# Linear attention and a gated MLP on one core: the first product's Strassen groups accumulate on copies in PSUM, with all operations in a new order

## The chip, the cores and the metric

The kernel runs on 1 core of one Trainium2 chip. A core has five engines, each of which works through its own queue in order: TensorE (PE, matmuls, with weight loads, PEld, that overlap them), VectorE (DVE), ScalarE (ACT), GpSimd (POOL) and SyncE (SP). They wait for each other through semaphores. SP and POOL here also issue the DMA transfers, which sixteen DMA engines carry out. Matmuls write to PSUM, which has 8 banks of 512 float32 columns on 128 partitions; DVE and ACT read and write it.

The metric is device time in microseconds (us), as the median of several executions. Before, it is 257.55 us (3 runs, 257.51 to 258.29).

## The reference

Two stages. The first is linear attention over 8 batches, 8 heads, 576 positions and head size 64; the second multiplies the 4608 x 512 result by two weight matrices with x * sigmoid(x) (silu) between them.

```python
def _attn_ref(q, k, v):
    q_s = np.exp(q - np.max(q, axis=-1, keepdims=True))
    q_s = q_s / (np.sum(q_s, axis=-1, keepdims=True) + 1e-09)
    k_s = np.exp(k - np.max(k, axis=2, keepdims=True))
    k_s = k_s / (np.sum(k_s, axis=2, keepdims=True) + 1e-09)
    kv = np.einsum('bhsd,bhse->bhde', k_s, v)
    return np.einsum('bhsd,bhde->bhse', q_s, kv)

def _moe_ref(x, w_in, w_out):          # x is the attention's output, 4608 x 512
    h = x @ w_in                       # w_in: 512 x 2048
    g = h * (1.0 / (1.0 + np.exp(-h)))
    return g @ w_out                   # w_out: 2048 x 512
```

## The kernel before

**Order.** The kernel defines some 800 named operations (`op(name, f, ...)` from L624 on) and then calls them in the order of the text `ORDER` (L18 to L67, run at L807). Each call appends instructions to the queues of the engines that it uses, so the order of the names is, engine by engine, the order of the instructions. No scheduler moves anything afterwards. The start (batch 0's attention, L545 to L621) is written out by hand ahead of the list.

**Attention, by batch b.** Names carry the batch, and .0 or .1 for the half of the heads.
- `lq`, `lk`, `lv` (load, L146) bring 576 KB of q, k or v each. Batch 0 is issued by SP, batches 1 and 2 by POOL, 3 to 7 by SP. Each of the three has two buffers, so a load waits until the buffer's last reader is done.
- `eq` and `ek` are the exponentials on ACT (L163, L168); `z` sums a row of q on DVE and takes its reciprocal (L207, L211); `n` multiplies by it, on POOL from batch 2 on (L216); `tq` (L226) is a DMA transpose of q, issued by SP; batch 0 and 1 are transposed by PE (`tr`, `tc`). `vc` casts v to bf16, on POOL from batch 2 on (L144).
- `kv` (L248, PE) multiplies k and v, `kc` normalizes the result on DVE. `X` (L282, PE; `xt` for chunk 1) forms the attention's output of a chunk of 512 rows, already transposed, in PSUM banks 0, 1, 6 and 7, and four `x` copies (ACT or DVE) bring it to SBUF.

**Weights.** `W1a` to `W1d` and `W2a` to `W2d` are loads by POOL (L564, L570) that also convert to fp16. `WS` and `T` are sums and differences of weight blocks on DVE (L373, L487).

**First 576 rows** (batch 0) go through both products plainly: `w` (PE, L307, 16 blocks of 128 hidden units), `h` and `v` (tanh on ACT, product on DVE), then `p0` to `p15` (PE, L445), which accumulate in banks 2 to 5. `p12` to `p15` read `W2d`. Chunk t = 1 has only 448 rows of its own; half its hidden units are plain, `m0` to `m7` (PE, L335) with `mu` (silu on ACT).

**Strassen chunks, t = 1 to 8.** Both products use the seven-product form of a 2 x 2 block multiplication. In the first product a group g (two per chunk, 1 then 0; chunk 1 has one) is made of products `g{t}.{g}.1` to `.7` (L425), each of eight matmuls of 256 columns, in the order 1, 2, 6, 5, 7, 4, 3. Products 1, 6, 7 and 4 accumulate in banks 0 and 1, one on top of the other. Products 2, and then 5 and 3, use a second pair of banks: 2 and 3 or 6 and 7. With P for product, the four results are C11 = P1 + P2, C12 = P1 + P6 + P5 + P3, C22 = P1 + P6 + P7 + P5 and C21 = P1 + P6 + P7 + P4. To get them, three copies of the growing sum (`s`, L142 on ACT or L144 on DVE; 128 x 1024 float32) are taken into SBUF, and three adds on DVE (`a`, L403) bring the other pair of banks to them. Four silus on ACT (`u`, L409) write the hidden values; three read the sums in SBUF, one reads banks 0 and 1.

Each copy must have read banks 0 and 1 before PE may add the next product to them; the list therefore puts other PE work in between, mostly the second product's products for the chunk before, `b{t}.{i}.{m}` (L503; eight matmuls of 256 columns each, banks 4 and 5). `S`, `sa` to `sc`, `wa` to `wl` and `o` are the second product's sums, copies, adds and stores; the last chunk's are called `e`.

Of the kernel before, what the change touches and what calls it, by code (L numbers as in the profile page):

```python
# [42 lines left out]
    b3.5.1 s4.0.1a S3.4 b3.7.0 vc6.1 u4.1.2 g4.0.7 z6.1 vc6.0 g4.0.5 s4.0.2a b3.7.1 a4.0.2 n6.1 g4.0.4 sc3
    u4.0.2 g4.0.3 wc3 n6.0 b3.3.0 u4.0.4 a4.0.1 b3.4.0 u4.0.0 X5.0 X5.1 kv6 x5.0a x5.1v tq6 x5.3a x5.2v
    b3.3.1 u4.0.1 xs5.1 g5.1.1 xs5.2 wb3 b3.4.1 s5.1.0v o2.1 ek7.1 g5.1.2 kc6 g5.1.6 wl3a xs5.3 xs5.4 a5.1.0
    lv7.0 b4.2.0 s5.1.1a lv7.1 b4.1.0 S4.1 eq7.1 g5.1.7 ek7.0 b4.2.1 s5.1.2v o3.1 g5.1.5 S4.2 b4.1.1 u5.1.0
    a5.1.2 g5.1.4 sa4 g5.0.2 o3.0 u5.1.4 wa4 g5.1.3 S4.3 u5.1.2 vc7.1 g5.0.1 b4.6.0 a5.1.1 vc7.0 s5.0.0a
    b4.6.1 a5.0.0 u5.1.1 g5.0.6 S4.4 b4.5.0 s5.0.1a b4.5.1 sb4 u5.0.0 g5.0.7 g5.0.5 s5.0.2v b4.7.0 eq7.0
    a5.0.2 b4.7.1 z7.1 g5.0.4 sc4 g5.0.3 b4.4.0 a5.0.1 u5.0.4 b4.4.1 wc4 u5.0.1 X6.0 X6.1 kv7 x6.0v u5.0.2
    x6.3v b4.3.0 x6.1a kc7 b4.3.1 x6.2a xs6.1 xs6.2 g6.1.1 xs6.4 wl4v g6.1.2 S5.1 s6.1.0a b5.1.0 a6.1.0  # L50
    g6.1.6 xs6.3 g6.0.2 wb4 s6.1.1a S5.2 b5.1.1 o4.0 b5.2.0 S5.3 g6.1.7 S5.4 b5.2.1 s6.1.2a z7.0 g6.1.5 sa5
    g6.1.4 wa5 n7.0 b5.6.0 a6.1.2 u6.1.4 b5.6.1 g6.0.1 n7.1 sb5 u6.1.0 g6.1.3 s6.0.0a b5.7.0 a6.1.1 tq7
    b5.7.1 a6.0.0 u6.1.1 g6.0.6 sc5 b5.5.0 s6.0.1a o4.1 g6.0.5 u6.1.2 g6.0.7 b5.5.1 s6.0.2v b5.4.0 wc5
    g6.0.4 a6.0.2 b5.4.1 u6.0.4 b5.3.0 u6.0.2 X7.0 X7.1 x7.0a x7.1v g6.0.3 x7.2a xs7.1 u6.0.0 g7.1.1 x7.3v
# [12 lines left out]
"""  # L67


@with_exitstack  # L70
def kernel(
    ctx: ExitStack,
    tc: tile.TileContext,
    q: bass.AP,
    k: bass.AP,
    v: bass.AP,
    w_in: bass.AP,
# [190 lines left out]
    def pieces(t):  # L268
        a, e = (S, 2 * TCH) if t == 1 else (t * TCH, (t + 1) * TCH)
        got = []  # L270
        while a < e:
# [3 lines left out]
            a += n  # L275
        return got

    def xt_mm(b, cc, col, n, bank, dst):
        for r in range(2):
            for s in range(2):  # L280
                h = slice(s * 64, (s + 1) * 64)
# [267 lines left out]
    for name, src in (("qt", q), ("kt", k)):  # L549
        load(0, name, src, 0, nc.sync)  # L550
        if name == "qt":
            load(0, name, src, 1, nc.sync)
# [286 lines left out]
```

## Time and profile before

| What | Value |
|---|---|
| median of 3 runs | 257.55 us |
| the profiled execution's own time | 258.61 us |
| its span, first to last instruction | 256.6 us |
| TensorE clock granted over the span | 1.0 |
| DVE adds of a group, 128 x 1024 (L403) | 42 of 1214 ns |
| ACT copies out of PSUM, 128 x 1024 (L142) | 29 of 1010 ns |
| DVE copies out of PSUM, 128 x 1024 (L144) | 13 of 1222 ns |
| ACT silu, from SBUF and from PSUM (L409) | 42 of 1056 ns, 14 of 1020 ns |
| ACT table loads | 16 of 1283 ns |
| read from HBM, written to HBM | 36.70 MB, 9.44 MB |

Times in the trace count from the span's start. "PE PS L445 <- DMA W" reads: PE, whose instruction on line 445 writes the tile PS, waited for the DMA that writes the tile W. The profile's busy time of PE is modelled, since matmuls are pipelined; whether PE lost time is seen in the distance from one matmul's start to the next. "Landing" is the time at which a transfer's semaphore tells that all its data are there.

### The profile page before, as it was taken

The page shows a single profiled execution, that of the slowest core. Times are in us where ns is not written, and L with a number is a line of the kernel's source. Part 1 is how long each engine was busy: PE and PEld are TensorE (multiplying, and loading weights), DVE is VectorE, ACT ScalarE, POOL GpSimd, SP SyncE. Part 2 cuts the span into 40 slices and gives each one's busy share as a digit, 9 for nine tenths or more (in the row PEclk, how much of TensorE's full clock was granted, in tenths as well). Part 3 has the DMA queues.
Part 4 walks back from the last instruction along what each step waited for, and adds up shares of the span by engine and source line. Part 5 has one row for each costly group of instructions (what it writes and reads, how often), then busy time and mean ns, then how long its engine had stood idle before and what let it go on. Part 6 is the DMA issues. An engine that isn't in the chain of part 4 may idle for free.

```text
span 256.6 us, 6459 instructions
## 1 busy us (share of the span) xinstructions
PE 249.1 (97%) x2732; PEld 204.2 (80%) x2732; DVE 206.2 (80%) x276; ACT 190.9 (74%) x225; POOL 65.8 (26%) x62
## 2 busy tenths in 40 slices
PE   8799999999999999999999999999999999999994
PEld 3457746656888888888888888888888888888883
DVE  2958999888999898998987986896579836886752
ACT  5766876699999999999879988737587665664411
POOL 1753593650450622350073030006000000000022
PEclk9999999999999999999999999999999999999999
DMA  7999999979959957996874960021807000600365
GB/s 248 348 181 297 302 301 283 351 140 393 378 128 213 403 187 137 361 335 168 276 266 68 224 236 3 3 52 32 163 14 153 13 0 4 148 18 0 66 141 123
DMA packets 36044, 45.89 MB, mean 179 GB/s; under 512 B 16288, under 2 KB 21088, under 8 KB 36016
## 3 DMA queue, kind: packets, MB, share of 16 engines
q1 hardware_dynamic: 29456, 33.56, 45.5%
q0 software_dynamic: 6160, 11.60, 17.8%
q10 hardware_dynamic: 400, 0.33, 0.6%
q8 instruction: 21, 0.34, 0.5%
q14 instruction: 7, 0.06, 0.1%
HBM read 36.70 MB, written 9.44 MB: 180 GB/s over the span
## 4 chain that ended last, share of the span: by engine, by line
PE 76%; DMA 11%; issue 5%; POOL 3%; ACT 2%; DVE 1%; ACTq 0%; POOLq 0%
PE PS L503 37%; PE PS L425 33%; DMA qt<-in_q_dram 5%; DMA kt<-in_k_dram 5%; PE PS L335 3%; PE PS L248 2%; PE PS L282 2%; POOL W L564 1%; DMA out_dram<-ow 1%; POOL qt L152 1%; DVE GT L323 1%; ACT L409 0%; POOL W L570 0%; ACT sg L320 0%; ACT GT L409 0%
## 5 line engine op out<-in xcount | busy, mean ns | idle before, releaser
L403 DVE TENSOR_TENSOR h<-PS,h 128x1024 f32<-128x1024 f32 (+1 forms) x45 | 54.2, 1206 | 9.3 <-PE PS L425 7.8
L503 PEld LDWEIGHTS <-GT 128*128 128x128 f16 x512 | 50.1, 98 | 5.9
L425 PEld LDWEIGHTS <-WS 128*128 128x128 f16 x480 | 46.7, 98 | 6.5 <-issue 0.6
L409 ACT ACTIVATE GT<-h 128x1024 f16<-128x1024 f32 (+1 forms) x45 | 46.8, 1051 | 0.9 <-DVE h L403 0.7
L503 PE MATMUL PS<-W,GT 128*128 128x256 f16 x384 | 47.3, 273 | 0.0
L425 PE MATMUL PS<-XS,WS 128*128 128x256 f16 (+1 forms) x360 | 45.0, 272 | 0.0
L142 ACT COPY h<-PS 128x1024 f32<-128x1024 f32 (+1 forms) x31 | 31.1, 1003 | 16.9 <-PE PS L425 15.7
L503 PEld LDWEIGHTS <-S 128*128 128x128 f16 x384 | 37.1, 98 | 4.6
L425 PEld LDWEIGHTS <-W 128*128 128x128 f16 x360 | 35.2, 98 | 4.4
L216 POOL TENSOR_TENSOR eq<-eq,rzq 128x1152 bf16<-128x1152 bf16 x13 | 27.3, 2115 | 37.6 <-DVE rzq L211 36.3
L503 PE MATMUL PS<-T,S 128*128 128x256 f16 x256 | 32.2, 273 | 0.0
L144 POOL CAST vaug<-vt 128x1152 bf16<-128x1152 f32 x12 | 15.8, 1328 | 61.5 <-DMA vt<-in_v_dram 61.4
L425 PE MATMUL PS<-XT,W 128*128 128x256 f16 (+1 forms) x240 | 29.7, 272 | 0.0
L144 DVE COPY h<-PS 128x1024 f32<-128x1024 f32 (+1 forms) x14 | 17.0, 1212 | 9.2 <-PE PS L425 4.4
L207 DVE TENSOR_REDUCE zq<-eq 128x18 f32<-128x1152 bf16 x14 | 18.8, 1342 | 4.1 <-ACT eq L163 4.0
L163 ACT ACTIVATE eq<-qt 128x1152 bf16<-128x1152 f32 (+1 forms) x18 | 18.9, 1055 | 3.1 <-DMA qt<-in_q_dram 2.8
L168 ACT ACTIVATE ek<-kt 128x1152 bf16<-128x1152 f32 x16 | 18.6, 1163 | 3.0 <-DMA kt<-in_k_dram 2.9
L791 POOL DMA_DIRECT2D out_dram<-ow x5 | 2.7, 545 | 70.0 <-DVE ow L773 70.0
L409 ACT ACTIVATE GT<-PS 128x1024 f16<-128x1024 f32 (+1 forms) x15 | 15.2, 1013 | 6.1 <-PE PS L425 6.1
L503 PE MATMUL PS<-T,GT 128*128 128x256 f16 x128 | 16.3, 272 | 0.0
L307 PE MATMUL PS<-XT,W 128*128 128x288 f16 x128 | 16.0, 286 | 0.2 <-DMA W<-in_moe_w_in_dram 0.2
L503 PE MATMUL PS<-W,S 128*128 128x256 f16 x128 | 16.1, 273 | 0.0
(85 smaller groups left out, 332.4 us busy)
## 6 DMA issues: line engine op xcount, KB each, us to landing
out_dram<-ow SPq DMA_DIRECT2D x64, 128.0 KB, 3.0
qt<-in_q_dram SPq DMA_DIRECT2D x11, 576.0 KB, 5.9
kt<-in_k_dram SPq DMA_DIRECT2D x11, 576.0 KB, 7.5
vt<-in_v_dram SPq DMA_DIRECT2D x11, 576.0 KB, 6.6
qt<-in_q_dram POOLq DMA_DIRECT2D x4, 576.0 KB, 11.4
kt<-in_k_dram POOLq DMA_DIRECT2D x4, 576.0 KB, 13.9
vt<-in_v_dram POOLq DMA_DIRECT2D x4, 576.0 KB, 12.6
W<-in_moe_w_in_dram POOLq DMA_DIRECT2D x3, 512.0 KB, 10.6
```

The source lines that it names most:

```text
L142: eng.copy(out=o, in_=i)
L144: eng.tensor_copy(o, i)
L163: nc.scalar.activation(out=half(st[b]["eq"], cc)[:, :, g0:g1], in_=jgd(b, "qt", cc)[:, :, g0:g1], func=ACT.Exp)
L168: nc.scalar.activation(out=half(ek, cc), in_=jgd(b, "kt", cc), func=ACT.Exp)
L207: nc.vector.reduce_sum(out=z, in_=e, axis=AX.X)
L216: eng.tensor_tensor(out=e, in0=e, in1=r[:, :, :, None].to_broadcast([128, J, 2, D]), op=ALU.mult)
L307: nc.tensor.matmul(out=PS[:, WIDE[fb] + n, 0:S // 2], lhsT=W1[:, c, fb * 128:(fb + 1) * 128], rhs=XTS[0][:, c, n * (S // 2):(n + 1) * (S / ...
L335: nc.tensor.matmul(out=PS[:, bank, o0:TCH], lhsT=W1[:, c, fb * 128:(fb + 1) * 128], rhs=XTS[t % 2][:, c, o0:TCH], start=(c == 0), stop=(c ...
L403: nc.vector.tensor_tensor(out=four(t, i), in0=group_bank(t, g), in1=four(t, i), op=ALU.add)
L409: nc.scalar.activation(out=group_out(t, f, n), in_=x, func=ACT.Silu, scale=1.0 / XS)
L425: nc.tensor.matmul(out=PS[:, bank + p // 2, (p % 2) * HT:(p % 2) * HT + width(t)], lhsT=a[:, c, p * 128:(p + 1) * 128], rhs=bb[:, c, 0:wid ...
L503: nc.tensor.matmul(out=PS[:, bank, m * HN:(m + 1) * HN], lhsT=a[:, fc, m * 128:(m + 1) * 128], rhs=bb[:, fc, :], start=(first and fc == 0) ...
```

## The change

It has three parts.

1. In chunks 2 to 8 a group keeps one of its running sums in PSUM. `s{t}.{g}.1` (`seed`) copies P1 from banks 0 and 1 to a pair of banks SB (2 or 6), and product 2 then accumulates on that copy, without a starting flag: C11 is complete there with no add. Product 5 goes to the other pair, SE (6 or 2). `s{t}.{g}.5` (`snap5`) copies it to SBUF; `a{t}.{g}.12` adds P1 + P6 to it and writes the sum back into SE, where product 3 accumulates on it: C12. `a{t}.{g}.22` adds P1 + P6 + P7 to the copy in SBUF: C22. C21 stays in banks 0 and 1. So a group has two copies and two adds in place of three and three, and three of four silus read PSUM. Chunk 1 keeps the old form. In `xt_mm` the starting flag is now set for the first piece of a chunk alone.
2. The start that was written out by hand becomes named operations of the list, and each `w` is split in two.
3. The list is a new one from end to end of its middle; the last part, from `e1.0` on, is as before.

The new functions and the changed parts of old ones:

```diff
-    def xt_mm(b, cc, col, n, bank, dst):
+    def xt_mm(b, cc, col, n, bank, dst, start=True):
...
+                    start=start,
+                    stop=True,
+                    skip_group_check=True,
...
     def group(t, g, i):
-        bank = 0 if i in (1, 6, 7, 4) else other(t, g)
+        if i in (1, 6, 7, 4):
+            bank = 0
+        elif t == 1:
+            bank = other(t, g)
+        else:
+            bank = SB[g] if i == 2 else SE[g]
+        fresh = (1, 2, 5) if t == 1 else (1, 5)
...
-                    start=(i in (1, 2, 5) and c == 0 and p % 2 == 0),
+                    start=(i in fresh and c == 0 and p % 2 == 0),
...
+    def pair(bank):
+        return PS[:, bank:bank + 2, :].rearrange("p b n -> p (b n)")
+    H5 = [None] * 2
+    def seed(g, eng):
+        copy(eng, pair(SB[g]), pair(0))
+    def snap5(g, eng):
+        H5[g] = mp.tile([128, 2 * TCH], FP32, name=f"h{g}", bufs=1)
+        copy(eng, H5[g], pair(SE[g]))
+    def add12(g):
+        nc.vector.tensor_tensor(out=pair(SE[g]), in0=pair(0), in1=H5[g], op=ALU.add)
+    def add22(g):
+        nc.vector.tensor_tensor(out=H5[g], in0=pair(0), in1=H5[g], op=ALU.add)
+    def silu4(t, g, x, f, n):
+        x = H5[g] if x is None else pair(x)
+        nc.scalar.activation(
+            out=group_out(t, f, n), in_=x.rearrange("p (f n) -> p f n", f=4), func=ACT.Silu, scale=1.0 / XS
+        )
+    SE = (6, 2)
+    SB = (2, 6)
...
-        op(f"w{fb}", wide_mm, fb, range(2 if fb in (0, 2) else 0, NC))
+        op(f"w{fb}.0", wide_mm, fb, (0, 1))
+        op(f"w{fb}.1", wide_mm, fb, (2, 3))
...
+            both(f"s{n}1", seed, g)
+            both(f"s{n}5", snap5, g)
+            op(f"a{n}12", add12, g)
+            op(f"a{n}22", add22, g)
+            op(f"u{n}11", silu4, t, g, SB[g], 4 * g + 8, 0)
+            op(f"u{n}12", silu4, t, g, SE[g], 4 * g + 8, 1)
+            op(f"u{n}21", silu4, t, g, 0, 4 * g, 0)
+            op(f"u{n}22", silu4, t, g, None, 4 * g, 1)
```

The list of before where the wide products begin (the two pieces w0.0 and w2.0 come from the hand-written start), and from the last pieces of W2 to the start of chunk 2:

```
    lk1.0 w1 lk1.1 w2 h1 w0 h2 v1 w3 h0 W2b1 w5 v0 v2 h3 w4 WS0.1 h5 w6 v3 h4 W2b2 v4 w7 v5 w8 h7 h6 v7 w9
...
    qp1a h13 v12 w14 eq1.1.1 v13 qp1b WS1.2 W2c1 p0 h14 z1.0 ek1.0 p1 z1.1.0 n1.0 z1.1.1 p2 h15 ek1.1 v15 p3
    WS1.4 W2c2 tr1.0 v14 lq2.0 p4 tc1.0a tc1.0b lq2.1 n1.1 p5 W2d p6 lk2.0 T1 vc1.0 lk2.1 p7 tr1.1 lv2.0
    vc1.1a vc1.1b gcopy WS1.3 kv1 lv2.1 tc1.1b p8 tc1.1a kc1 WS0.3 xt1.0 xt1.1 x1.0a x1.1v p9 x1.2a x1.3v
    g1.1.1 xs1.1 xs1.2 xs1.4 g1.1.2 s1.1.0a WS0.4 p10 xs1.3 eq2.0 a1.1.0 p11 eq2.1 z2.0 g1.1.6 g1.1.5
    s1.1.1a z2.1 n2.0 p12 ek2.0 g1.1.7 p13 s1.1.2v n2.1 ek2.1 p14 a1.1.2 g1.1.4 p15 tq2 u1.1.4 g1.1.3 po2v
    vc2.1 po1a m0 po3v po0a a1.1.1 u1.1.0 vc2.0 m1 lk3.0 mu0 m2 T2 lq3.0 mu1 lq3.1 m3 u1.1.2 lk3.1 T3 m4
    lv3.0 u1.1.1 lv3.1 m5 T4 mu2 os0 mu4 kv2 mu5 m6 mu3 kc2 X2.0 mu6 X2.1 x2.0v m7 x2.1a x2.3a x2.2v g2.1.1
```

The same parts of the new list:

```
    kc0.1 heat3 x0.0a x0.0v X0.1 w0.0 w2.0 x0.1v w1.0 x0.1a w0.1 h0 w3.0 WS0.1 v0 w1.1 h1 w2.1 v1 w3.1 w4.0 w4.1 h2
...
    w15.0 h13 qp1a w15.1 w14.0 h12 eq1.1.0 h15 v13 v12 eq1.1.1 z1.1.0 qp1b z1.0 w14.1 p0 p1 WS1.1 p2 p3 ek1.1 W2c1
    lq2.0 WS1.2 WS0.3 z1.1.1 h14 vc1.0 v15 ek1.0 p4 v14 p5 n1.0 p6 n1.1 tr1.0 tc1.0a p7 tr1.1 tc1.0b W2c2 vc1.1b
    vc1.1a tc1.1b kv1 p8 gcopy lq2.1 kc1 lk2.1 tc1.1a WS1.4 xt1.0 W2d xt1.1 x1.0a x1.1v p9 x1.2a g1.1.1 lk2.0 x1.3v
    eq2.0 g1.1.2 xs1.1 xs1.2 p10 s1.1.0a g1.1.6 lv2.0 eq2.1 xs1.3 z2.0 p11 lq3.0 a1.1.0 s1.1.1a xs1.4 z2.1 g1.1.5
    ek2.1 lq3.1 g1.1.7 s1.1.2v a1.1.2 p12 lv2.1 ek2.0 n2.0 vc2.0 T1 p13 g1.1.4 g1.1.3 T3 p14 u1.1.4 n2.1 p15 WS0.4
    po0a a1.1.1 po2v po1a vc2.1 u1.1.0 lk3.1 m1 T2 tq2 m0 m3 mu1 m2 mu0 u1.1.1 m5 m4 po3v mu3 lv3.1 mu5 mu2 kv2 m7
    kc2 mu4 u1.1.2 X2.0 vc3.1 X2.1 x2.0v x2.1a x2.3a x2.2v m6 mu7 mu6 xs2.1 eq3.0 g2.1.1 eq3.1 lk3.0 b1.1.0 os3
```

One group of chunk 3 (t = 3, g = 0) before, and after:

```
    sb2 lq5.1 g3.0.1 u3.1.2 a3.1.1 lv5.1 lk6.0 b2.7.0 s3.0.0a
    o1.0 S2.4 b2.2.1 u3.1.1 a3.0.0 g3.0.6 lv6.0 b2.7.1 s3.0.1v eq5.0 g3.0.5 wa2 g3.0.7 sc2 lq6.0 z5.0 b2.4.0
    s3.0.2a lk6.1 b2.5.0 vc5.1 eq5.1 a3.0.2 g3.0.4 o1.1 n5.0 z5.1 g3.0.3 u3.0.4 b2.5.1 a3.0.1 n5.1 u3.0.0
...
    z4.1 b2.6.0 u3.1.12 n4.1 u3.1.11 g3.0.1 b2.6.1 s3.0.1a g3.0.5 u3.1.22 sb2 S2.3 g3.0.2 vc5.1 g3.0.6 lk6.0 o1.0
    b2.7.1 u3.0.11 b2.7.0 s3.0.5v a3.0.12 ek5.0 sc2 lq5.0 g3.0.7 g3.0.3 tq4 vc5.0 u3.0.12 wa2 a3.0.22 lv6.1 b2.4.0
    g3.0.4 b2.4.1 X4.1 kv5 u3.0.21 X4.0 u3.0.22 S2.4 x4.1v wl2v b2.5.0 lk6.1 x4.0a x4.3v kc5 g4.1.1 x4.2a b3.1.0
```

## The prediction

> **What bounds the kernel now.** I read the page's head, the 40 slices, PE's waits, the chain of waits and then the timelines of 47 to 65 us.
>
> ```profile
> span 256.6 us, 6459 instructions
> PE 249.1 (97%) x2732; PEld 204.2 (80%) x2732; DVE 206.2 (80%) x276; ACT 190.9 (74%) x225; POOL 65.8 (26%) x62
> ...
> DMA  7999999979959957996874960021807000600365
> ...
> PE 76%; DMA 11%; issue 5%; POOL 3%; ACT 2%; DVE 1%; ACTq 0%; POOLq 0%
> ```
>
> PE is busy nearly throughout. The DMA digits are near 9 over the first eight slices (to 51 us).
>
> ```profile
> PE PS L234 <- DVE eq L216: 1.3, 2, 0.9
> PE PS L561 <- DVE XS L546: 1.2, 1, 1.2
> PE PS L335 <- ACT GT L409: 0.6, 1, 0.6
> PE PS L445 <- DMA W<-in_moe_w_out_dram: 0.3, 1, 0.3
> PE PS L307 <- DMA W<-in_moe_w_in_dram: 0.2, 1, 0.2
> ```
>
> These are all PE waits that the profile names (total, times, longest). None is in the Strassen chunks from X2 on. Counted from start to start of matmuls, a product of eight 256-column matmuls takes 0.873 us there, and no start after 62 us is over 0.31 us late (those few stand where PE changes between 64-row and 128-row work). So from X2.0 at 60.36 us on the kernel is one packed row of PE work. Removing DVE or ACT work there gains nothing; X2.0's start decides the end.
>
> What holds X2.0 is the loading of batch 2:
>
> ```profile
> 36.84 0.80 POOL W L570
> ...
> 38.30 12.31 DMA kt<-in_k_dram
> ...
> 51.87 1.28 ACT L409
> ...
> 53.16 0.93 ACT GT L409
> ...
> 54.13 4.70 PE PS L335 x24
> ```
>
> (Chain of waits: start, length.) The k load issued at 38.30 lands at 50.61; its exp, a table load and a silu follow, and the plain product m0 starts at 54.13, late by the 0.76 us that stand in its matmul starts.
>
> ```profile
> 47.62 0.59 PE L445 MATMUL PS<-W,GT 128*128 128x512 f16 x2 [0.30 <-DMA W<-in_moe_w_out_dram]
> ...
> 47.47 4.19 POOL L216 TENSOR_TENSOR eq<-eq,rzq 128x1152 bf16<-128x1152 bf16 x2 [6.88 <-DVE rzq L211]
> 54.20 3.26 POOL L144 CAST vaug<-vt 128x1152 bf16<-128x1152 f32 x2 [2.54 <-DMA vt<-in_v_dram]
> ...
> 51.68 3.35 SPq L226 DMA_TRANSPOSE qT<-eq  x1
> 55.22 0.43 SPq L152 DMA_DIRECT2D kt<-in_k_dram  x1
> 55.76 0.92 SPq L152 DMA_DIRECT2D qt<-in_q_dram  x2
> ```
>
> p12 waits for the last W2 piece. POOL does n2.0 and n2.1 (47.47 to 51.66) before it waits for v; SP sends the transpose tq2 at once, and only then batch 3's loads. POOL's queue holds a backlog: by the records of issue and landing its loads land one after another, W2c1 39.10, W2c2 40.39, lq2.0 41.91, lq2.1 45.68, W2d 47.58, lk2.0 49.09, lk2.1 50.61, lv2.0 52.07, lv2.1 54.07; a 576 KB load takes 1.46 to 1.52 us of it.
>
> **The change, part by part.** *Elementwise passes, t = 2 to 8.* 14 groups lose two passes each, an add and a snap. By the order list the 42 copies of before (29 on ACT, 13 on DVE) become 28 (22 and 6), the 42 adds 28. So DVE loses 14 adds of 1214 ns (L403 row) and 7 copies of 1222, together 25.6 us; ACT 7 copies of 1010, and 28 silus read PSUM (1020 ns) in place of SBUF (1056): 8 us. Value on the path: 0, since PE waits for neither there. Matmuls are the same in number and shape: 0.
>
> *New waits.* Before, every copy out of bank 0 has at least two products (1.75 us) of other PE work between the product that it reads and the one that overwrites; I counted the order list and found 1.75 to 2.62 us at all 42 places. After, seed, add12 and add22 have 1.75 us or more at all places too (1.75 at most of the adds), and PE queues nothing else behind them. The tightest kind fits: the DVE snap of 62.95 to 64.17 was followed by P6 at 64.31, so 0.14 us are left over. At four places (t = 4 and 5) snap5 and add12 in series, 1.01 + 1.21, have 2.62 us, which leaves 0.4 for three handoffs: 0 to 0.1 each. DVE now has 31 of 42 handovers (28 adds, 3 seeds) where it had 13, so a late DVE instruction is felt more often, but it is less busy. Value 0, at worst +0.4.
>
> *PSUM as destination.* No row shows a pass that writes PSUM. Bounds: 1.01 us (ACT, same elements, out of PSUM) and 2.17 us (L487, T3 written in place, the slowest DVE pass of the trace). I take 1.21, the same pass to SBUF. At 2.17, 14 add12 would each overrun 1.36 by up to 0.8 us: +11 us; at 1.01 nothing is gained.
> The Trainium skill's ScalarE: Activation LUTs says, beside its table of limits, that ScalarE writes PSUM faster than SBUF; no run so far shows it, and by it the 11 ACT seeds would only be better covered, which leaves the sum as it is.
>
> *Wide products.* w1.0 now stands before w0.1, so the wait for W1's second piece (0.36 us between starts at 16.07) shrinks to 0.1; the next piece, landing at 19.10, then costs 0.1. About 0.3 us gained by p0. It is spent again: kv1 needs batch 1's last v load, which has the same loads ahead of it and lands at 37.99; with ACT's half cast (0.67) behind tc1.0a it can start its second half at 39.2, against kv1 at 39.31 before. Value at xt1: 0.
>
> *Loads of batch 2.* On POOL's queue lk2.1 now goes ahead of W2d. By the landings, lk2.1 47.2, W2d 49.1, lk2.0 50.6, the v loads as before. p12 comes one group later (47.6) and would wait for 49.1; five products' time (5.0 us) on, m1 would start at 54.1, where m0 started at 54.13. ACT's chain: lk2.0 50.6, exp 1.16, table 1.28, silu 0.92: 54.0. Still 0.
>
> *Loads of batch 3.* This decides. SP's order before was tq2, lk3.0, lq3.0, lq3.1. Now it is lq3.0, lq3.1, lk3.1, tq2. lq3.0 waits only for eq2.0 (41.9 + 1.16 = 43.1), lq3.1 for eq2.1 (about 47), lk3.1 for ek2.1 (about 50). So three loads of 1.46 us come onto engines that the records show occupied all the time, while W2d, lk2.0 and lv2.0 are still queued. A load that goes in between moves what is left by its own time.
>
> *n2.1 behind vc2.0.* POOL's order is now n2.0, vc2.0, n2.1, vc2.1. So the transpose waits for v: landing of lv2.0, cast 1.33, n2.1 2.11, then tq2 (4.7 us from issue to landing). Without the batch 3 loads: 52.07 + 1.33 + 2.11 + 0.1 + 4.7 = 60.3, just at X2.0's 60.36. So the cover of this step is exactly used up, and each microsecond that lv2.0 comes later is a microsecond for X2.0, kv3 and all after.
>
> **Sum.** lv2.0 with none, one, two or three loads in front: X2.0 at 60.3, 61.8, 63.2, 64.7, that is 0, +1.5, +2.9, +4.4. I take two: lq3.0 and lq3.1 are issued 9 and 5 us before 52.07, and the first load's 3.6 us from issue to landing (0.74 to 4.36 on the page's clock) leaves both time; lk3.1 at 50 comes for the end only. PE's other road, ACT's chain with lk2.0 at 53.6, gives m1 at 57.1 and X2.0, 6.2 later as before, at 63.3: the same. Everything after is packed and moves along: +2.95 us on the profiled execution (258.61 us, span 256.6 and 2.0 around it), 261.6. The profiled one is 1.06 above the median; on the median, 257.55 + 2.95 = 260.5.
>
> How the engines share two queues is the weak step. The only row of it is at 10.5 to 11.5 us, where SP's last load kept its 1.46 us while POOL's first packets came in: SP's queue was not made to wait. The Trainium skill's DMA: Bandwidth & Descriptors (Queues, rings and completion order) says that each engine goes round-robin between its queues, packet by packet. By that a 16-packet SP load per engine would be through while 16 POOL packets pass, and the sum is the same two loads.
>
> **Rivals.**
> *The loads don't hold each other up* (0.13): q3 slips into gaps, as the third slice's 181 GB/s, against 283 to 351 in others, may suggest; against it, the engines are recorded busy in it at 9 tenths. Then X2.0 is at 60.3 to 60.5 and the time 257.6, same. Here too belongs the case that the passes go away and nothing else changes.
> *Faster* (0.14). One mechanism: batch 2's loads land earlier than in this trace, and the new order has then taken away PE's waits of 16 to 54 us. lq2.1 took 3.8 us where its neighbours take 1.5, so one engine lagged by over 2 us; without that lag m1 comes as soon as PE is ready. Gain at most 0.36 + 0.28 + 0.46 + 0.76 = 1.86 us (late starts at w1, tr1.0, p12, m0): 255.7. It decides where lv2.0 lands by 50.3 despite the q loads. For it: the three runs lie 0.3 to 1.1 below the profiled one. Against it: SP's order.
> *Passes into PSUM don't fit* (0.08): 0.25 us over the cover at 14 add12 is +3.5 on top of the collision: 264; to 272 at the far bound.
> *Only some late starts of 0.3 to 1 us at kv3 and kv4* (0.03), whose v loads now follow tq2 and n3: 258.4 to 259.
>
> **How the numbers follow.** The forecast has 0.62: 260.5, own range 258.6 to 262.8 (one load to three, with kv3 late by up to 1). The whole range takes in the no-collision case and stops short of the faster one's best and the PSUM case: 257.0 to 262.8, which leaves out about 0.18. A measurement of this kernel can tell about 0.3%, 0.77 us, from no change. Slower 0.62 + 0.08 + 0.03 = 0.73, same 0.13, faster 0.14.
>
> **What would show it.** Right: SP's q loads of batch 3 issued before 50 us, lk2.0 and lv2.0 landing 2 to 4 us later than 49.1 to 50.6 and 52.1, POOL's n2.1 after 56 us, X2.0 at 62 to 65 us, and from there PE starts again 0.873 us per product, with the end as far behind X2.0 as before (196 us). DVE's busy time down by some 25 us, ACT's by some 8, and no PE wait on DVE after X2. Wrong: X2.0 before 61 us, or late starts of PE in the chunks, then at g3, g7 and g4 behind the adds.

## The result, and the profile after

The changed kernel takes 265.00 us (median of 4 runs, 264.07 to 265.22), the kernel before beside it 257.53 (4 runs): ratio 1.0278, 95% interval 1.0245 to 1.0311. It is slower by 7.5 us, where 3 were forecast. The profiled execution took 264.93 us, its span is 263.1; that of before took 258.61, one microsecond above its median, with a span of 256.6.

The page of the changed kernel, head and busy times:

```profile
span 263.1 us, 6451 instructions
## 1 busy us (share of the span) xinstructions
PE 251.1 (95%) x2732; PEld 204.3 (78%) x2732; DVE 191.5 (73%) x255; ACT 182.6 (69%) x218; POOL 69.2 (26%) x62
...
PE 56%; DVE 20%; DMA 9%; ACT 7%; POOL 3%; issue 3%; SPq 1%; ACTq 0%; DVEq 0%; POOLq 0%
```

DVE is busy 15 us less and ACT 8. The prediction had some 25 for DVE: it runs fewer instructions, but some of them now take longer. And in the chain of waits DVE's share went from 1% to 20%: PE's 76% are down to 56%. POOL, which does the same work as before, is busy 3.4 us longer.

The costliest groups (operation, tiles, shapes, count, busy us, mean ns), first of the changed kernel, then of the one before:

```profile
L456 DVE TENSOR_TENSOR PS<-PS,h 128x1024 f32<-128x1024 f32 x14 | 17.2, 1230 | 13.9 <-PE PS L433 8.4
L459 DVE TENSOR_TENSOR h<-PS,h 128x1024 f32<-128x1024 f32 x14 | 17.1, 1219 | 10.4 <-PE PS L433 10.4
L215 POOL TENSOR_TENSOR eq<-eq,rzq 128x1152 bf16<-128x1152 bf16 x13 | 31.0, 2394 | 57.1 <-DVE rzq L210 50.3
```

```profile
L216 POOL TENSOR_TENSOR eq<-eq,rzq 128x1152 bf16<-128x1152 bf16 x13 | 27.3, 2115 | 37.6 <-DVE rzq L211 36.3 <-DVE rzq L196 0.7 <-ACT GT L409 0.5
```

The add that writes PSUM (L456) takes 1230 ns, the one that writes SBUF (L459) 1219: PSUM as a destination costs next to nothing. But the same 13 multiplications on POOL (`n`) take 2394 ns on average in place of 2115. Where does PE lose time? Its longest waits, by the profile:

```profile
PE PS L538 <- DVE ow L558: 1.6, 1, 1.6
PE PS L589 <- DVE XS L581: 1.2, 1, 1.2
PE PS L233 <- DVE eq L215: 1.0, 2, 0.5
PE PS L538 <- DVE GT L512: 1.0, 1, 1.0
PE PS L433 <- DVE h L143: 0.6, 1, 0.6
```

All five are waits for DVE; the second, at the very start, is in the kernel before too (L561). A start of a matmul is called late by the distance from the start ahead of it, less what that kind takes when matmuls follow without a wait. Counted so, PE's late starts come to some 23 us after and 16.5 before; the difference is about that of the spans (6.5). Of the 6.5 us, 2.0 are there when X2.0 starts (62.37, before 60.36), and 4.5 come after it. The large late starts that are new: 0.66 at `w4.0`, which starts as its weights W1b land (19.54), 0.69 and 0.66 at `tr1.0` and `tr1.1`, 0.71 and 0.36 at `g1.1.4` and `g1.1.3`, 0.45 and 0.55 ahead of X2.0 (at `m7` and at X2.0 itself), 1.15 at `b1.7.0`, 0.51 at X3.0, 0.66 within X6, 1.72 at `b5.2.0`. At eight of these eleven (all but `w4.0`, X3.0 and X6) an instruction on DVE that is far longer than its kind stands ahead of the late matmul. The timeline of DVE at the two largest (start, length, engine, line):

```profile
76.03 2.87 DVE L512 TENSOR_TENSOR GT<-GT 128x2048 f16<-128x2048 f16 x1
...
177.40 1.31 DVE L512 TENSOR_TENSOR S<-GT 128x2048 f16<-128x2048 f16 x1
178.74 3.02 DVE L512 TENSOR_TENSOR S<-S,GT 128x2048 f16<-128x2048 f16 x1
181.69 1.21 DVE L512 TENSOR_TENSOR GT<-GT 128x2048 f16<-128x2048 f16 x1
```

and of POOL at the same times:

```profile
75.69 2.12 POOL L215 TENSOR_TENSOR eq<-eq,rzq 128x1152 bf16<-128x1152 bf16 x1 [1.12 <-DVE rz L258]
...
175.51 5.17 POOL L215 TENSOR_TENSOR eq<-eq,rzq 128x1152 bf16<-128x1152 bf16 x2 [17.91 <-DVE rzq L210]
```

`S1.3` and `S5.2` take 2.87 and 3.02 us, their kind 1.16 to 1.22. Each starts while POOL runs an `n`, and ends 1.1 us after that `n` (77.81 and 180.68): it stood until POOL was almost done and then took its own time. And `n7.0`, the second of the two in the last line, which began at 177.58 beside `S5.1` (177.40 to 178.71), is 3.1 us long in place of 2.1: it stood until that one was done. The other long ones are `WS1.2` (33.38, 2.48 us; its kind 0.68) beside `n1.0` (which runs on POOL too, although it is batch 1's), `xs1.4` (47.54, 1.68; 0.39) beside `n2.0`, and `T3` (54.02, 3.02; 1.22) and `WS0.4` (56.97, 1.64; 0.68) beside `n2.1` and `vc2.1`. All have two inputs, both in SBUF.

That is theory T1: **a DVE instruction with two SBUF inputs and a POOL instruction that reads SBUF don't run side by side; the later one stands until the other ends.** The Trainium skill's SBUF — State Buffer (Who interferes with whom) says the same: a DVE instruction with two SBUF inputs contends with a GpSimd instruction that reads SBUF, not with one that only writes it, and the one that issues second is blocked for the whole of the other.

### The profile page after: what moved, and what is told of

It reads as the page before. It is cut to its first block, busy times and chain, and to the rows that moved or that the text cites. A ratio compares the mean times of both kernels' runs of the same rounds, so it can differ in the third digit from the quotient of the medians.

```text
span 263.1 us, 6451 instructions
## 1 busy us (share of the span) xinstructions
PE 251.1 (95%) x2732; PEld 204.3 (78%) x2732; DVE 191.5 (73%) x255; ACT 182.6 (69%) x218; POOL 69.2 (26%) x62
## 4 chain that ended last, share of the span: by engine, by line
PE 56%; DVE 20%; DMA 9%; ACT 7%; POOL 3%; issue 3%; SPq 1%; ACTq 0%; DVEq 0%; POOLq 0%
PE PS L538 26%; PE PS L433 22%; DMA qT<-eq 5%; PE PS L309 4%; DMA vt<-in_v_dram 4%; DVE zq L206 3%; POOL eq L215 3%; DVE S L512 2%; DVE WS L375 2%; PE PS L281 2%; DVE XS L385 1%; ACT eq L162 1%; DVE GT L325 1%; PE PS L247 1%; DVE W L522 1%
## 5 line engine op out<-in xcount | busy, mean ns | idle before, releaser
L463 ACT ACTIVATE GT<-PS 128x1024 f16<-128x1024 f32 x42 | 41.0, 1023 | 21.0 <-PE PS L433 20.8
L215 POOL TENSOR_TENSOR eq<-eq,rzq 128x1152 bf16<-128x1152 bf16 x13 | 31.0, 2394 | 57.1 <-DVE rzq L210 50.3
L433 PE MATMUL PS<-XT,W 128*128 128x256 f16 (+1 forms) x240 | 30.7, 272 | 0.0
L456 DVE TENSOR_TENSOR PS<-PS,h 128x1024 f32<-128x1024 f32 x14 | 17.2, 1230 | 13.9 <-PE PS L433 8.4
L459 DVE TENSOR_TENSOR h<-PS,h 128x1024 f32<-128x1024 f32 x14 | 17.1, 1219 | 10.4 <-PE PS L433 10.4
L143 DVE CAST XT<-PS 128x512 f16<-128x512 f32 (+1 forms) x17 | 11.2, 679 | 12.5 <-PE PS L281 10.1
L141 ACT COPY h<-PS 128x1024 f32<-128x1024 f32 (+1 forms) x13 | 12.9, 996 | 4.5 <-PE PS L433 4.1
```

Source lines behind the costliest of these rows:

```text
L141: eng.copy(out=o, in_=i)
L143: eng.tensor_copy(o, i)
L215: eng.tensor_tensor(out=e, in0=e, in1=r[:, :, :, None].to_broadcast([128, J, 2, D]), op=ALU.mult)
L433: nc.tensor.matmul(out=PS[:, bank + p // 2, (p % 2) * HT:(p % 2) * HT + width(t)], lhsT=a[:, c, p * 128:(p + 1) * 128], rhs=bb[:, c, 0:wid ...
L456: nc.vector.tensor_tensor(out=pair(SE[g]), in0=pair(0), in1=H5[g], op=ALU.add)
L459: nc.vector.tensor_tensor(out=H5[g], in0=pair(0), in1=H5[g], op=ALU.add)
```

## The experiments

The ratios are to the kernel before, run on the same chip. The late starts are from each kernel's one profiled execution.

### e1: batch 3's loads behind tq2, as before the change

```diff
-    ... xs1.3 z2.0 p11 lq3.0 a1.1.0 s1.1.1a xs1.4 z2.1 g1.1.5 ek2.1 lq3.1 g1.1.7 ... lk3.1 m1 T2 tq2 m0 m3 ...
+    ... xs1.3 z2.0 p11 a1.1.0 s1.1.1a xs1.4 z2.1 g1.1.5 ek2.1 g1.1.7 ... m1 T2 tq2 lq3.0 lq3.1 lk3.1 m0 m3 ...
```

> The changed kernel with batch 3's loads lq3.0, lq3.1 and lk3.1 moved behind the transpose tq2 on SP, as before the change; nothing else. The prediction's theory (these loads push batch 2's back by two loads of 1.46 us): lv2.0's landing moves forward by up to 2.9 us, X2.0 from 62.37 to about 59.5 to 60.5, the time from 265.0 to about 262.1. Theory T1 (VectorE instructions with two SBUF inputs and POOL instructions that read SBUF stand still beside each other; the loads of the two queues don't hold each other up): POOL's loads land within 0.5 us of where they did (lv2.0 51.59), X2.0 within 0.5 us of 62.37, the time 264.5 to 265.5.

Measured: 264.86 us, ratio 1.0304 (1.0242 to 1.0366). `lv2.0` lands at 51.31 (51.59 in the changed kernel), X2.0 starts at 62.22. So the collision that the prediction is built on is not what costs the time. In the changed kernel SP issues these loads near the times that were predicted:

```profile
44.89 2.23 SPq L151 DMA_DIRECT2D qt<-in_q_dram  x2
49.18 0.37 SPq L151 DMA_DIRECT2D kt<-in_k_dram  x1
55.99 2.81 SPq L225 DMA_TRANSPOSE qT<-eq  x1
```

but by the records of landing they took 8.6, 8.4 and 7.4 us (53.45, 55.12, 56.60). By the trace's DMA packets, SP's queue moved nothing until 48.46, 3.6 us after the first of these loads was issued, while POOL's queue moved its own. From then on both moved, and POOL's last two loads, `lv2.0` and `lv2.1`, landed 2.36 and 2.25 us behind the one ahead (51.59 and 53.84), in e1 1.48 and 1.47 (51.31 and 52.78). So the queues do share, but late: `lv2.0` lands 0.28 us later than in e1 and `lv2.1` 1.06, and not 2.9, and X2.0 is where it was. Here too `tq2` is issued 1.3 us sooner than in the changed kernel, and it buys nothing: `n2.1` now meets the weight difference `T1` (an operation, not the theory), which takes 3.14 us, in place of `T3`, and DVE has the same delay.

### e2: wb4 ahead of S5.2

```diff
-    ... b4.3.1 S5.1 u6.1.12 b4.3.0 u6.1.22 S5.2 sa5 s6.0.1a S5.3 s6.0.5a g6.0.2 wb4 g6.0.6 a6.0.12 b5.2.0 ...
+    ... b4.3.1 S5.1 u6.1.12 b4.3.0 wb4 u6.1.22 S5.2 sa5 s6.0.1a s6.0.5a g6.0.2 g6.0.6 a6.0.12 S5.3 b5.2.0 ...
```

> The changed kernel with VectorE's order changed at one place of the body: the copy wb4 ahead of S5.2, and S5.3 two VectorE instructions later, so that no S lies beside POOL's n7.1 with work behind it that PE waits for. T1: b5.2.0, 1.72 us late in the changed kernel (S5.2 took 3023 ns beside n7.1, in place of 1160), is on time, X7.0 and all that follows 1.7 us earlier, the time 263.3 (263.0 to 263.7). The rival (the four-pass form's handovers are too tight everywhere, and VectorE's stretched instructions are only where idle time collects): the lateness turns up at the next groups, the time stays at 264.5 to 265.5.

Measured: 263.27 us, 1.73 less than the changed kernel; ratio 1.0230 (1.0179 to 1.0281). `wb4` frees the bank that `b5.2.0` writes, and in the changed kernel it stood on DVE behind `S5.2` and `S5.3`. Now `b5.2.0` is on time, and the lateness turns up nowhere behind it. (The `n` that the expectation calls n7.1 is n7.0.) That the medians differ by just the 1.72 is in part chance: the four runs of e2 lie between 262.26 and 265.38.

### e3: n on DVE

```diff
-    op("n1.0", qnorm, 1, 0, nc.gpsimd)
+    op("n1.0", qnorm, 1, 0, nc.vector)
...
-                op(f"n{b}.{c}", qnorm, b, c, nc.gpsimd)
+                op(f"n{b}.{c}", qnorm, b, c, nc.vector)
```

> The changed kernel with all qnorm multiplications (n) issued on VectorE in place of POOL; the order list is the same, VectorE has about 20 us more to do. T1: the S, T, WS and XS instructions keep their own length (1.16 to 1.22, 0.69, 0.41 us) at the places where n ran (33.4, 47.5, 54.0, 76.0, 178.7 us), PE's late starts behind them (0.69, 0.71, 0.45, 1.15, 1.72 us) are gone, less what the queue of VectorE now adds: the time 260 to 263. The rival (VectorE's load and the handovers of the four-pass form decide): 20 us more on VectorE make it later, 265 to 270.

Measured: 272.77 us, ratio 1.0594 (1.0538 to 1.0651): T1's expectation missed. `WS1.2`, `xs1.4`, `S1.3` and `S5.2` do have their own length, but the operations `T1` and `T3`, which now run beside POOL's casts, take 2.18 and 2.06 us. DVE is busy 203.5 us in place of 191.5, and `b1.7.0` is late by the same 1.15: an `n` in DVE's own queue holds up what is behind it as much as standing beside POOL does. b5.2.0 is 1.10 late, X3.0 0.93, g5.1.7 0.94, and the transposes come late too:

```profile
PE PS L281 <- DMA qT<-eq: 4.1, 4, 2.5
```

(PE's longest wait, where the changed kernel has 0.3.) The time is beyond the rival's 270, too. This run does not tell T1 from its rival; e9 was made for that.

### e4: the mechanism by itself

Behind the last operation of the kernel before, six DVE instructions of one kind, alone and beside five POOL instructions (T1, T2 and W1 in the comments are weight tiles):

```diff
+    for pool in (None, pool_read, pool_write):       # nothing; tensor_copy vaug <- ek; memset
+        for dve in (dve_pair, dve_one, dve_psum):    # T1 - T2; T2 * constant; PSUM + W1
+            meet()
+            for _ in range(6):
+                dve()
+                if pool is not None and _ < 5:
+                    pool()
```

> The kernel before with a measurement behind its last operation: six VectorE instructions of one kind (subtract with two SBUF inputs; multiply of one SBUF input by a constant; add of a PSUM and an SBUF input) alone, then beside POOL copies that read SBUF, then beside POOL memsets that only write it. T1: the subtract with two SBUF inputs goes from some 1.2 us to the length of POOL's copy and more beside the copies, and keeps it beside the memsets; the add with one PSUM input is the same in all three; for the multiply by a constant T1 says nothing sure, either. The rival (stretched by SBUF traffic in general): all three kinds are lengthened, beside the memsets too. The output isn't touched; the time is that of the kernel before and some 60 to 120 us.

The subtract with two SBUF inputs, alone, beside copies, beside memsets (count, then shortest, middle and longest in ns, first and last start):

```profile
L811 DVE TENSOR_TENSOR S<-T,T x6: 1203/1226/1226, 252.0 to 258.3; 128x2048 f16<-128x2048 f16 x6
...
L811 DVE TENSOR_TENSOR S<-T,T x6: 1225/2056/2067, 272.6 to 283.0; 128x2048 f16<-128x2048 f16 x6
...
L811 DVE TENSOR_TENSOR S<-T,T x6: 1203/1224/1226, 301.3 to 307.6; 128x2048 f16<-128x2048 f16 x6
```

Beside copies, which take 1150 ns alone, both engines go to 2.03 to 2.06 us: they take turns, but for some 0.3 us by which the two lengths together (2.38) are over that. Beside memsets nothing happens. For the other two kinds, the whole of the six (start, length; alone, then beside copies, then beside memsets for the multiply):

```profile
259.92 4.31 DVE L814 TENSOR_SCALAR S<-T 128x2048 f16<-128x2048 f16 x6
...
264.65 7.49 DVE L817 TENSOR_TENSOR W<-PS,W 128x1024 f16<-128x1024 f32 x6
...
284.60 8.51 DVE L814 TENSOR_SCALAR S<-T 128x2048 f16<-128x2048 f16 x6
...
293.46 7.49 DVE L817 TENSOR_TENSOR W<-PS,W 128x1024 f16<-128x1024 f32 x6
...
309.16 7.79 DVE L814 TENSOR_SCALAR S<-T 128x2048 f16<-128x2048 f16 x6
```

The add with one PSUM input (L817) takes 1224 ns in all three. The multiply of one SBUF input by a constant (L814) goes from 694 ns to 1526 beside copies and to 1399 beside memsets. So T1 holds for the instructions that it speaks of, and the rival (SBUF traffic in general) falls with the add, which reads one SBUF input and writes SBUF.

### e5: the head's sums moved off POOL's reads

```diff
-    lq2.0 WS1.2 WS0.3 z1.1.1 ... n1.0 p6 n1.1 tr1.0 ... xs1.3 z2.0 ... s1.1.1a xs1.4 z2.1 ... n2.0 vc2.0 T1 p13
-    g1.1.4 g1.1.3 T3 p14 u1.1.4 n2.1 p15 WS0.4 po0a a1.1.1 po2v po1a ... po3v mu3 ...
+    lq2.0 z1.1.1 ... n1.0 p6 n1.1 WS1.2 tr1.0 ... tc1.1b WS0.3 ... xs1.3 xs1.4 z2.0 ... s1.1.1a z2.1 ... n2.0 n2.1 vc2.0 T1 p13
+    g1.1.4 g1.1.3 p14 u1.1.4 p15 po0a a1.1.1 po2v T3 po1a ... po3v WS0.4 mu3 ...
```

> The changed kernel with the order of its first 57 us changed so that VectorE's sums with two SBUF inputs (WS1.2, WS0.3, xs1.4, T3, WS0.4) don't stand beside POOL's n and vc: the sums go a few operations later, n2.1 goes ahead of vc2.0. T1: the 2482, 1681, 3024 and 1635 ns instructions come back to 0.69, 0.41, 1.22 and 0.68 us each (or stand where nothing waits), PE's late starts at tr1.0 (0.69), g1.1.3 and g1.1.4 (0.71 and 0.36) and before X2.0 (0.45 and 0.55) shrink, X2.0 comes 1.5 to 2.9 us earlier than the changed kernel's 62.37; the body keeps its own losses (1.15 at b1.7.0, 1.72 at b5.2.0): 262.3 (261.8 to 263.5). The prediction's theory (loads of batch 3): batch 3's loads are as before on SP, so X2.0 stays within 0.5 of 62.37 and the time at 264.5 to 265.5.

Measured: 262.47 us, 2.5 less than the changed kernel; ratio 1.0178 (1.0144 to 1.0213). T3 takes 1.22 us, WS0.4 0.68, and X2.0 starts at 58.82. The profiled execution was the slowest of the four (264.70) and shows where a gain of the head can go:

```profile
74.10 9.73 DMA qT<-eq
83.93 0.10 ACT eq L162
84.03 1.08 issue
85.11 1.28 ACT L463
86.40 1.95 ACT GT L463 x2
88.39 0.40 PE PS L281 x6
```

(Chain of waits.) The transpose `tq3`, issued at 74.10, lands after 9.7 us, behind two loads and four stores on SP's queue. ACT's `eq4.0` waits for it, since `eq` has one buffer, and three silus and X3.0 stand behind `eq4.0`: 3.57 us late in this execution.

### e6: lq4.1 behind the transpose

```diff
-    u2.1.21 b1.6.1 lq4.1 u2.1.12 ... tq3 ... lv4.0 eq4.0 z4.0
+    u2.1.21 b1.6.1 u2.1.12 ... tq3 ... lv4.0 lq4.1 eq4.0 z4.0
```

> The kernel of e5 with one more move: batch 4's load lq4.1 from ahead of the transpose tq3 on SP to behind lv4.0. In e5 X2.0 came 3.55 us earlier than in the changed kernel, but X3.0 waited 3.57 us: tq3, issued at 74.10, landed only at 83.82, behind lq4.1 (68.99 to 78.93) and four stores, and ScalarE's eq4.0 stood 4.42 us for it with three silus behind it. Theory T2 (the transposes queue behind loads on SP's own DMA queue, so the gain of the head is given back there): tq3 lands near 80.9, X3.0 is 0.3 to 1.0 late in place of 3.57, the time 259.7 (259.2 to 260.7). The rival (tq3 is bound by its issue behind n3.1, or eq4.0's wait isn't what holds X3.0): X3.0 stays 3 or more late, the time 262 to 263.

Measured: 262.30 us, ratio 1.0196 (1.0151 to 1.0241). `tq3` lands 5.2 us after its issue and X3.0 is on time, as theory T2 says. The time is T2's miss: it is that of e5, and falls in the rival's range. e5's profiled execution was 2.2 above its median, so its 3.57 is no typical value; in e6's, X2.0 came at 60.81, after 0.77 at p12 and 0.84 at m1. How much of the head's gain the transposes take back differs from one execution to the next. `tq2` has the trouble of `tq3`: with `n2.1` ahead of `vc2.0` it is issued at 49.84 in e5 and 50.26 in e6, but behind the loads of batch 3 on SP's queue it takes 8.6 and 10.4 us to land, where it took 4.7 in the changed kernel (issued at 55.99) and in e1 (ahead of those loads).

### e7: the body's sums moved as well

```diff
-    ... b1.6.0 z3.0 a2.1.22 g2.1.4 wa1 ... n3.0 S1.3 g2.0.1 ... s5.1.1v S3.4 b3.4.1 ... g5.1.7 xs5.4 g5.1.3 ...
+    ... b1.6.0 S1.3 a2.1.22 g2.1.4 wa1 z3.0 ... n3.0 g2.0.1 ... s5.1.1v b3.4.1 ... g5.1.7 xs5.4 S3.4 g5.1.3 ...
```

and the moves of e2.

> The kernel of e6 with the body's sums moved off POOL's n and vc as well: S1.3 ahead of a2.1.22 (z3.0 behind wa1 for it), wb4 and S5.3 as in e2, S3.4 behind xs5.4. T1: b1.7.0 (1.14 late in e5), b5.2.0 (1.72) and g5.1.7 (0.87) are on time, so 3.0 to 3.7 less than e6: 256.0 (255.2 to 257.2), level with the kernel before or up to 2 us under it, since the new head reaches X2.0 1.5 us sooner than the old one. The rival (the four-pass form's handovers cost something of their own): the late starts move on to other groups and the time stays above 258.5.

Measured: 261.47 us, ratio 1.0148 (1.0120 to 1.0177): T1's time was missed by 5.5 us, and it falls in the rival's range. b1.7.0 and b5.2.0 are on time, g5.1.7 0.25 late. In their place are g2.0.5 (0.59: `kc3` now stands behind two `z` on DVE), X3.0 (0.99: `n3.1` and `tq3` later), kv4 (0.51: `lv4.0` behind `tq3`), g3.1.5 (0.55: `n4.0` meets `S2.1`, 2568 ns), X6 (0.60: `tq6`).

### e8: the same loss made in the kernel before

```diff
-    ... b5.2.0 S5.3 g6.1.7 S5.4 b5.2.1 s6.1.2a z7.0 g6.1.5 sa5 g6.1.4 wa5 n7.0 b5.6.0 a6.1.2 ...
+    ... b5.2.0 S5.3 g6.1.7 b5.2.1 s6.1.2a z7.0 g6.1.5 sa5 g6.1.4 wa5 S5.4 n7.0 b5.6.0 a6.1.2 ...
```

> The kernel before with one move: VectorE's S5.4 from ahead of z7.0 to behind wa5, so that it meets POOL's n7.0 while the add a6.1.2 waits behind it. Same instructions, same six-pass groups. T1: S5.4 stands until n7.0 ends and takes about 2.0 us in place of 1.16, a6.1.2 goes from 176.0 to about 177.3 and PE's g6.0.1 behind it is 1.3 us late: 258.7 (258.2 to 259.2). The rival (no standing still; only the order counts): S5.4 takes 1.2 us, a6.1.2 is 0.4 late at most: 257.4 to 257.9.

Measured: 258.03 us against 257.32 (ratio 1.0042, 1.0020 to 1.0065), between the two forecasts. The trace decides:

```profile
173.60 2.45 DVE L477 TENSOR_TENSOR S<-GT,S 128x2048 f16<-128x2048 f16 x1
175.97 1.21 DVE L403 TENSOR_TENSOR h<-PS,h 128x1024 f32<-128x1024 f32 x1
```

`S5.4` takes 2.45 us (1.22 at its old place) beside an `n` of 172.85 to 174.97, and the matmul behind the add is 0.81 late, the only new late start after X2.0.

### e9 and e10: POOL as busy, but only writing

```diff
+        if eng is nc.gpsimd:
+            eng.tensor_copy(e[0:1, 0, 0, 0:1], r[0:1, 0, 0:1])
+            for _ in range(2):
+                eng.memset(e, 0.02)
+            return
```

in `qnorm`, in the changed kernel (e9) and in the one before (e10).

> The changed kernel, with POOL's n (qnorm, from n1.0 on) replaced by instructions that keep POOL busy as long and wait for the same reciprocal, but read no SBUF beyond one element: a one-element copy and two memsets of the same half of eq. Left out: the division of q's exponentials by their sum (q's part of the output is that of a constant). Order, form, loads and all other instructions as in the changed kernel. T1 (VectorE's sums with two SBUF inputs stand beside a POOL instruction that reads SBUF, not beside one that writes it): the 2482, 1681, 3024, 2866 and 3023 ns instructions are back at 0.69, 0.41, 1.2, 1.2 and 1.2 us; the late starts at tr1.0 (0.69), g1.1.4 (0.71), b1.7.0 (1.15) and b5.2.0 (1.72) are gone or nearly so; the time 260.5 (259.5 to 262). The rival (form or order, POOL being busy at all): the time stays at 264.5 to 265.5.

> The same replacement of n in the kernel before (the same part of the output left out). T1: only two VectorE instructions stand beside an n or a cast there, with nothing of PE waiting for them, so there is little to gain: 257.4 (256.5 to 257.8). The rival (the replacement shortens the road to the transposes by itself, whatever VectorE does): it gains about as much here as in the changed kernel, 4 us.

e10 measured 257.36 us against 257.18 (1.0009, 0.9990 to 1.0028): nothing to gain there, as expected. e9 measured 263.49, ratio 1.0280 (1.0203 to 1.0356): by its interval no different from the changed kernel; T1's time is missed by 3, and it falls between T1's range and the rival's. But in its trace the sums that run beside an `n` have their own length, `WS1.2` (0.69), `xs1.4` (0.38), and `S1.3` and `S5.2`:

```profile
74.58 2.18 POOL L218 MEMSET eq<- 128x1152 bf16 x2
...
74.68 1.22 DVE L517 TENSOR_TENSOR GT<-GT 128x2048 f16<-128x2048 f16 x1
...
177.89 1.22 DVE L517 TENSOR_TENSOR S<-S,GT 128x2048 f16<-128x2048 f16 x1
```

(the multiplications' memsets first, then `S1.3`, then `S5.2`), and tr1.0, tr1.1, g1.1.4, b1.7.0 and b5.2.0 are on time. So the standing still is shown, with the order left as it was and POOL busy about as long. `T3` and `WS0.4` tell nothing here: `T3` ran before `n2.1` began, and `WS0.4` took 1.64 us beside `vc2.0`, a cast that still reads. What takes its place is 0.78 at m1, 1.48 within X2.0, 1.43 at X3.0, 0.97 at g5.1.7 (`S3.4` beside a `vc`, 2.20 us, which still reads) and 0.51 at g5.0.4. The one within X2.0 is the end of this chain:

```profile
52.43 0.02 POOL vaug L143
52.45 1.16 issue
53.61 0.65 POOL eq L216
54.26 0.05 issue
54.31 1.06 POOL eq L218
...
56.51 4.72 DMA qT<-eq
61.23 0.04 issue
61.27 0.58 PE PS L286 x12
```

`vc2.0` first, then `n2.1`'s place, then the transpose, 4.7 us. So there are two causes, one behind the other: DVE and POOL standing beside each other, and transposes that come late by the new order.

### e11 and e12: the rest, by order alone

e11 is e7 with moves for each of its late starts; e12 undoes three that cost more than they gave, and moves `S1.4`. From e7 to e12:

```diff
-    ... S1.3 a2.1.22 g2.1.4 wa1 z3.0 ... z3.1 kv3 lk4.1 kc3 ... n3.1 ... T4 tq3 b1.4.0 S1.4 b1.4.1 vc4.1 a2.0.22 g2.0.4
-    lv4.0 lq4.1 eq4.0 z4.0 ... n4.0 ... wb1 ek5.1 a3.1.12 ... z4.1 ... n4.1 ... sb2 S2.3 ... S4.2 ... a5.0.12 ... S4.3 ...
+    ... S1.3 a2.1.22 g2.1.4 wa1 z3.0 ... kv3 lk4.1 kc3 z3.1 ... vc4.1 n3.1 ... T4 lv4.0 tq3 b1.4.0 b1.4.1 a2.0.22 S1.4 g2.0.4
+    lq4.1 ... wb1 ek5.1 eq4.0 S2.3 a3.1.12 ... z4.0 z4.1 ... n4.0 n4.1 ... sb2 ... a5.0.12 S4.2 ... a5.0.22 S4.3 ...
```

> The kernel of e7 with its remaining late starts after X2.0 addressed one by one, by order alone: kc3 ahead of z3.1 (g2.0.5, 0.59 late in e7); eq4.0, z4.0 and n4.0 moved behind chunk 2's silus, so that ScalarE's silus don't stand behind the transpose tq3 (X3.0, 0.99) and n4.0 doesn't meet S2.1 (g3.1.5, 0.55); vc4.1 ahead of n3.1 and lv4.0 ahead of tq3 (kv4, 0.51); S4.2 and S4.3 behind n6.0 and n6.1, so that tq6 goes earlier (X6, 0.60). T1 and T2 together (sums beside POOL's reads, transposes behind loads: nothing else is lost to the change): 2.5 to 3.2 less than e7, 258.6 (257.6 to 259.6), level with the kernel before within 1 to 2 us. The rival (the four-pass form costs something of its own): new late starts of the same size at the groups' adds and seeds, 260.5 to 262.

e11 measured 261.18 us (1.0172, 1.0138 to 1.0205), a miss, in the rival's range: the five late starts that it was aimed at are gone, and three of 0.65, 0.98 and 1.59 are new. In e11 one operand of chunk 3's `b3.1` is read before it is written.

> The kernel of e11 with the three moves undone that made late starts of their own there (u3.1.22 back to its place, where chunk 3's product b3.1 finds its operand written, which it did not in e11; ek5.1 and lk6.0 back to theirs; late starts of 0.98 at b2.4.0 and 1.59 at g4.1.7), and S1.4 behind a2.0.22, since vc4.0 met it in e11 (2172 ns in place of 1215, 0.65 late at g2.0.4). ScalarE's silu u3.1.21 now goes behind one exp more (1.1 us), which may make g3.0.1 0.5 to 0.9 late. T1 and T2: 2.3 to 2.7 less than e11, 258.6 (257.8 to 259.5). The rival (the four-pass form costs something of its own): the late starts move to other groups, 260.5 or more.

e12 measured 258.48 us (12 runs, before 257.36; ratio 1.0046, 1.0022 to 1.0071), as T1 and T2 expected and 2 us under the rival's. Its page:

```profile
span 256.4 us, 6452 instructions
## 1 busy us (share of the span) xinstructions
PE 249.4 (97%) x2732; PEld 204.0 (80%) x2732; DVE 184.2 (72%) x255; ACT 182.2 (71%) x218; POOL 65.9 (26%) x62
...
PE 72%; DMA 12%; ACT 5%; DVE 3%; issue 3%; POOL 3%; SPq 1%; ACTq 0%; DVEq 0%; POOLq 0%
```

With the changed kernel's groups and its adds into PSUM, 6.5 of its 7.5 us are back by order alone. (e12 moves sums, loads and transposes, so it does not tell how much of this belongs to each of the two causes.) DVE is busy 7.3 us less than in the changed kernel with the same instructions, and POOL 3.3 us less (before: 65.8): that is, nearly all of it, time in which they stood. No kernel here is faster than the one before: DVE is busy 22 us less in e12 than there, and it gains nothing, since PE is 97% busy in both.

## Why the prediction was wrong

The sign was right, but by luck: X2.0 came at 62.37, inside the 62 to 65 that the prediction named as its sign, for another reason, and 4.5 of the 6.5 us came after X2.0, where it saw none. The size was off by 4.5 us, and the mechanism was another. Of the other signs, the early issue of SP's loads and ACT's 8 us came. `lk2.0` and `lv2.0` landing 2 to 4 us late, `n2.1` after 56 (it began at 52.84), DVE's 25 us and no PE wait on DVE after X2 did not.

- *Elementwise passes, value 0*: right. With fewer passes nothing is gained, and with the tighter handovers little is lost: e12, which has all of them, is 1.1 us above before.
- *PSUM as destination, 1.21 us*: right, 1.23 (and ACT's copies take 1013 ns into PSUM, 1012 into SBUF). The upper bound of 2.17 was a misread row. Before's `T3` had been caught beside a cast, as these two lines of the kernel before show (DVE's timeline, then POOL's):

```profile
56.36 2.17 DVE L487 TENSOR_TENSOR W<-W 128x2048 f16<-128x2048 f16 x1
...
54.20 3.26 POOL L144 CAST vaug<-vt 128x1152 bf16<-128x1152 f32 x2 [2.54 <-DMA vt<-in_v_dram]
```

In e5 the same `T3` takes 1.22. The row was the mechanism of this case, in plain view, and was taken for the price of writing in place.
- *Loads of batch 3: "This decides"*: the step that failed. Two loads of 1.46 us were to push `lv2.0` to 55; it landed at 51.59, sooner than before (52.07). With the three loads moved behind `tq2` (e1) it landed at 51.31, 0.28 sooner and not 2.9, and the time stayed. SP's loads had moved nothing for their first 3.6 us. By the round-robin rule of the Trainium skill's DMA: Bandwidth & Descriptors (Queues, rings and completion order), which the prediction weighed, they would have shared as soon as both queues had work. Those 3.6 us do not agree with it, unless SP's packets were not yet at the engines, which the trace doesn't tell; the later spacing of 2.36 and 2.25 us does. Where these loads do cost something is on SP's own queue, once `tq2` is issued early behind them (e5, e6).
- *n2.1 behind vc2.0, transposes at 60.3*: right as a chain, and not what held X2.0 in the changed kernel. `tq2` landed at 60.71, X2.0 started at 62.37, since PE, ACT and DVE itself (`kc2`) were late behind `T3` and `WS0.4`. With the standing still gone (e9) this chain is what is left: X2.0 waits within itself until 61.27.
- *Wide products, value 0 at xt1*: wrong by 1.4 us (xt1.0 at 42.40 for 40.99). `p0` was to come 0.3 sooner than before and came 0.3 later (31.36 for 31.02), since `w4.0` waited 0.66 for W1b, where 0.1 was forecast. The rest is `WS1.2` beside `n1.0`, then `n1.1` behind it, `tr1.0` and `tr1.1` late.
- *"Everything after is packed and moves along"*: wrong. It was read from before's trace and carried over to a list in which everything after is in a new order. b1.7.0 and b5.2.0 alone cost 2.9 us; e2 took back the 1.72 of one with two DVE instructions moved.
- The moved sums (WS, T, S, xs) were costed at nothing, and no work was named that hides them. That is the term that was missing: 0.69 + 0.66 + 0.71 + 0.36 + 0.45 + 0.55 + 1.15 + 1.72 = 6.3 us of late starts behind them in the profiled execution. With X3.0 and X6 (0.51 + 0.66) and w4.0 (0.66), and without the 1.86 that before has at w1, tr1.0, p12 and m0 and the new kernel has not, that is 6.3 of the 6.5 between the spans. It is no price that comes back when it is taken away: in e9 it is gone, and the transposes take most of its place.

What stays open: how the last 1.1 us of e12 split. Its late starts that before lacks are small (0.26 at g1.1.5, 0.38 within X2.0, 0.30 at g2.1.7, 0.23 at g3.0.1), and one execution of each kernel varies by as much. In e12 X2.0 starts at 59.16 and waits within itself until `tq2` has landed (59.51, 9.5 us after its issue); `tq2` ahead of batch 3's loads was not tried in this order. And why SP's queue moved nothing for 3.6 us was not tried.

## What to carry to other kernels

When an order list is redone, check each two-SBUF-input DVE instruction against what POOL does at that time: move it where POOL is idle or only writes, or let it read PSUM, and put what PE waits for ahead of it. (A multiply by a constant is no way out: in e4 it is lengthened beside a writing POOL instruction too.) An instruction in the old trace that takes twice what its kind takes is a finding, not a price: look at the neighbouring engine before using it as a bound. And a stretch that is packed in the old order says nothing of the same stretch in a new one.

## What the runs showed of the hardware

- DVE (two SBUF inputs) and POOL (reading SBUF) take turns, nearly whole instructions at a time: 1226 and 1150 ns become 2056 and 2031 (e4). A DVE add with one input in PSUM is not touched (1224).
- A DVE multiply of one SBUF input by a constant, fp16, is: 694 ns alone, 1526 beside copies, 1399 beside memsets that read nothing. The Trainium skill's SBUF — State Buffer (Who interferes with whom) lists `tensor_scalar` among those that can lock both shared ports; the runs agree.
- Three loads that SP issued while POOL's queue had a backlog took 8.6, 8.4 and 7.4 us, and no packet of theirs moved for the first 3.6 us. Issued in e1 after POOL's had landed, the first two took 4.3 and 5.2. While both queues moved, POOL's loads landed 2.36 and 2.25 us apart, in e1 1.48 and 1.47.
- The DMA transpose of q took 4.7 us from issue to landing with nothing or little ahead of it on SP's queue (`tq2` before, in the changed kernel and in e1), and 8.6, 10.4 and 9.5 behind batch 3's loads (e5, e6, e12).
